# Rows of y scattered straight to their expert's part of DRAM, in place of a table of lists and gathers, on one Trainium2 core

## The chip, the cores and the metric

One NeuronCore of a Trainium2 chip runs the whole kernel. The metric is the device time in microseconds (us). All data is float32.

## The reference

A Fourier filter along the sequence (GFNet mixing), followed by a mixture of experts in which every row goes to one expert:

```python
# x: (8, 2496, 256); filt_r, filt_i: (1249, 256)
X = np.fft.rfft(x, axis=1)
y = np.fft.irfft(X * (filt_r + 1j * filt_i)[None], n=2496, axis=1).reshape(19968, 256)

logits = y @ w_gate                          # (19968, 8)
e = np.argmax(logits, axis=1)                # one expert for each row
gate = softmax(logits)[arange(N), e]
h = np.maximum(y @ w1[e], 0.0)               # w1: (8, 256, 1024)
out = gate[:, None] * (h @ w2[e])            # w2: (8, 1024, 256)
```

The reference sorts the rows by expert, multiplies each expert's rows with its weights, and puts the rows back in their order.

## The kernel before

**Fourier part.** The length 2496 is split into 39 x 64 (`N1` x `N2`). For each of the 8 batches there are four stages. Stage A (`stage_a`, DFT over 39) writes `zo` tiles to `zd` in DRAM. Stage B (`stage_b`) loads `zd` back in another order, multiplies with twiddles on TensorE and with the filter in four VectorE operations. Stage C (`stage_c`) writes `uo` tiles to `ud` in DRAM. Stage D (`stage_d`) loads `ud` and makes y, four of 22 columns of 117 rows at a time, in tiles `yo`. y goes to `yd` in DRAM. `turn_y` transposes y, `logits` multiplies it with the gate weights (result in the PSUM tile `lt`), the small copy `ls` takes that out, and `turn_logits` turns it back so that `lg` holds eight logits for each row. `zo`, `uo` and `yo` are allocated from one ring of six tiles (tag `st`). Loads of x, z and u share a ring of `NIN` = 8 tiles (`fin`).

**Routing.** After the last column of a batch, `route` works on all 22 columns: maximum, one-hot `oe` of the expert, softmax sum, and the rank of each row within its expert. The rank takes two matmuls on `oe` (`rk`: one with a triangle, one with ones) and a scan. The row of `table` (a DRAM tensor with a part for each expert) is that rank plus the rows counted so far (`cnt`). For each of the 22 columns, GpSimd then scatters 117 rows of 12 bytes to the table (L512: number of the output row, gate, number of the row in `yd`). `tile_map` then computes, on VectorE, which expert and which place of the table each tile of 512, 256 or 128 rows has (`erow`, `rrow`).

**Experts.** There are 65 tiles. For each, `listed` loads the tile's part of the table to `idt` (SP reads `rrow` into a register and waits for the batch's scatters), `gather` fetches the rows of `yd` by GpSimd with one indirect DMA for each 128 rows (L613), `turn_x` transposes them (`xT`), `hidden` does 8 steps of w1 with a ReLU, and `result` does w2, multiplies by the gate from `idt` and scatters 128 rows to the output by GpSimd (L668). Weights are loaded by SP, 1 MB at a time, into two `w1t` and two `w2t` tiles. The last 128-row tiles take w2 from a resident copy `w2s`, and w1 from four tiles.

**Order.** The order of PE, VectorE (DVE), ScalarE (ACT) and SP is written out by the program. `slot(k)` lists the steps of one time slot: stages B and C of batch k, stage A of batch k + 1, stage D and the logits of batch k - 1, each with a cost in us. The main loop takes such a step or an expert step, by a credit and by planned due times; after each it flushes the delayed stores (`move`), starts loads, advances the routing by two pieces (`side`) and issues expert loads (`prefetch`). `either` gives a copy out of PSUM to VectorE or ScalarE by planned load. GpSimd has its own order, in which the DMAs were issued.

In the trace the slots of stage B for batches 1 and 2 run from 77.7 to 141.0 us and from 141.0 to 209.3 us; from about 1047 us on only expert work is left.

Of the kernel before, what the change touches and what calls it, by code (L numbers as in the profile page):

```python
# [19 lines left out]
P = 128  # L20
# [112 lines left out]
def kernel(  # L133
# [40 lines left out]
    YB = TP * NG  # L174
    yd = dram.tile([B * YB + 1, D], F32, tag="yd", name="yd")

    table = dram.tile([TR, 3], I32, tag="table", name="table")
# [28 lines left out]
    seg = cst.tile([P, E, NG], F32, name="seg")  # L206
    fill = cst.tile([P, 3], I32, name="fill")
    yrow = cst.tile([TP, NG], I32, name="yrow")
# [45 lines left out]
    def load_rest():  # L254
        nc.sync.dma_start(out=tds, in_=td)
        nc.vector.memset(wg, 0.0)
        nc.sync.dma_start(out=wg[:, :, :E], in_=moe_w_gate.rearrange("(i p) e -> p i e", p=P))
        nc.sync.dma_start(out=ids0, in_=ids)
        nc.sync.dma_start(out=vld, in_=valid)
        zrow = sb.tile([P, 2, D], F32, tag="yw", name="zrow")  # L260
        nc.vector.memset(zrow[:1, 0], 0.0)
        nc.sync.dma_start(out=yd[B * YB:B * YB + 1, :], in_=zrow[:1, 0])

    def make_constants():
# [5 lines left out]
        nc.gpsimd.memset(seg, 1.0)  # L270
        nc.gpsimd.memset(seg[:, :, 0:1], 0.0)
        nc.gpsimd.memset(cnt, 0.0)
        nc.gpsimd.memset(fill[:, 0:1], N)
        nc.gpsimd.memset(fill[:, 1:2], 0)
        nc.gpsimd.memset(fill[:, 2:3], B * YB)
        nc.gpsimd.iota(yrow, pattern=[[1, NG]], base=0, channel_multiplier=NG)
# [19 lines left out]
    NIN = 8  # L296
# [36 lines left out]
    def stage_a(b, c):  # L333
        i0, n = CH[c]
        xt = ins.pop(("x", b, c))
        zo = sb.tile([TP, 4, D], F32, tag="st", name="zo", bufs=6)
# [28 lines left out]
    def stage_c(b, f):  # L365
        ys = outs.pop(("y", b, f))
        j = f % 4
        if j == 0:
            outs["u", b] = sb.tile([P, 4, D], F32, tag="st", name="uo", bufs=6)
# [16 lines left out]
    def stage_d(b, c):  # L386
        if c == 0:
            lgs[b] = sb.tile([TP, NG, E], F32, tag="lg", name="lg")
        i0, n = CH[c]
        ui = ins.pop(("u", b, c))  # L390
        yo = outs["o", b, c] = sb.tile([TP, 4, D], F32, tag="st", name="yo", bufs=6)
        for j in range(0, n, 2):
            p = bank()
            for i in range(2):

                k = N1 if i0 + j + i == NG - 1 else TP
                mm(p[:TP, i * D:(i + 1) * D], lhsT=tds[:k, i0 + j + i, :], rhs=ui[:k, j + i, :],  # L397
                   start=True, stop=True)
            evac(yo[:, j:j + 2, :], p[:TP, :].rearrange("p (i d) -> p i d", i=2), 512)
        move(yd[b * YB:(b + 1) * YB, :].rearrange("(r i) d -> r i d", i=NG)[:, i0:i0 + n, :], yo[:TP, :n])  # L400

    def turn_y(b, c):
        yo = outs.pop(("o", b, c))
# [33 lines left out]
    scatters, rows_at = {}, {}  # L437


    def route(b):  # L440
        lg = lgs.pop(b)
        sh3 = (TP, NG, E)
        she = (TP, E, NG)
        mx = sb.tile([TP, NG], F32, tag="mx", name="mx", bufs=1)
        nc.vector.tensor_reduce(mx, lg, axis=AX.X, op=ALU.max)
        oh = sb.tile([TP, NG, E], F32, tag="oh", name="oh", bufs=1)
        ex = sb.tile([TP, NG, E], F32, tag="ex", name="ex", bufs=1)
# [6 lines left out]
        idx = sb.tile([TP, NG], F32, tag="idx", name="idx", bufs=1)  # L454
        nc.vector.tensor_reduce(idx, oh, axis=AX.X, op=ALU.min)

        nc.vector.tensor_tensor(idx, idx, vld, op=ALU.mult)
        yield
        oe = sb.tile([TP, E, NG], F32, tag="oe", name="oe", bufs=1)
# [3 lines left out]
        pay = sb.tile([TP, NG, 3], I32, tag="pay", name="pay", bufs=1)  # L463
        sd = sb.tile([TP, NG], F32, tag="sd", name="sd", bufs=1)
# [4 lines left out]
        mm(rk[:TP, 0, :], lhsT=tri, rhs=oef, start=True, stop=True)  # L469
        mm(rk[:, 1, :], lhsT=ones, rhs=oef, start=True, stop=True)  # L470
        nc.vector.tensor_scalar(sd, in0=sd, scalar1=1e-9, scalar2=None, op0=ALU.add)
        nc.vector.reciprocal(pay.bitcast(F32)[:, :, 1], sd)
        yield
        nc.vector.tensor_scalar(pay[:, :, 2], in0=yrow, scalar1=float(b * YB), scalar2=None, op0=ALU.add)
        nc.vector.tensor_scalar(pay[:, :, 0], in0=ids0, scalar1=float(b * S), scalar2=None, op0=ALU.add)
        run = sb.tile([P, E, NG], F32, tag="run", name="run", bufs=1)
        runf = run.rearrange("p e t -> p (e t)")
        nc.vector.tensor_tensor_scan(
            runf, seg.rearrange("p e t -> p (e t)"), rk[:, 1, :], 0.0, op0=ALU.mult, op1=ALU.add
# [3 lines left out]
        pos = sb.tile([TP, E, NG], F32, tag="ex", name="pos", bufs=1)  # L483
        posf = pos.rearrange("p e t -> p (e t)")
        nc.vector.tensor_tensor(posf, runf[:TP], rk[:TP, 1, :], op=ALU.subtract)
        nc.vector.tensor_tensor(posf, posf, rk[:TP, 0, :], op=ALU.add)
# [6 lines left out]
        rowf = sb.tile([TP, NG], F32, tag="rowf", name="rowf", bufs=1)  # L493
        nc.vector.tensor_reduce(rowf, pos.rearrange("p e t -> p t e"), axis=AX.X, op=ALU.add)
        yield
        row = sb.tile([TP, NG], U32, tag="row", name="row", bufs=1)
        nc.vector.tensor_copy(row, rowf)  # L497
        nc.vector.tensor_tensor(cnt, cnt, run[:, :, NG - 1], op=ALU.add)
        yield
        rows = [(row[:N1 if t == NG - 1 else TP, t:t + 1], pay[:N1 if t == NG - 1 else TP, t, :]) for t in range(NG)]  # L500
        if b == B - 1:
# [5 lines left out]
            nc.vector.tensor_copy(pad, padf)  # L507
            rows += [(pad[:, e:e + 1], fill) for e in range(E)]
        scatters[b] = []
        rows_at[b] = pool(now[0] + 5.0, len(rows)) + 3.0  # L510
        for t, (at, what) in enumerate(rows):
            sc = nc.gpsimd.indirect_dma_start(  # L512
                out=table,
# [8 lines left out]
            scatters[b].append(sc.ins.name)  # L522
            yield
# [62 lines left out]
    work, idt, xgs, xts, w1t, w2t, hs = [], {}, {}, {}, {}, {}, {}  # L586
# [6 lines left out]
    def listed(i):  # L593
        n, e, r, b = work[i]
        r0 = nc.sync.value_load(r, min_val=0, max_val=TR - n * P)
        idt[i] = moe.tile([P, 4, 3], I32, tag="idt", name="idt", bufs=6)
        ld = nc.sync.dma_start(
            out=idt[i][:, :n], in_=table[bass.ds(r0, n * P), :].rearrange("(p i) c -> p i c", i=n)
        )
        tc.add_to_no_dep_group("listed", ld.ins)  # L600
        for name in scatters.pop(b, ()):
            tc.add_manual_dep(
                ld.ins, name, mybir.DependencyInfo(mybir.DependencyClass.Sync, mybir.DependencyReason.DATA),
                reason="the table is written for all batches so far",
            )

    def gather(i):
        n, e, r, b = work[i]
        xgs[i] = moe.tile([P, 4, D], F32, tag="xg", name="xg")

        rows = (b + 1) * YB if b < B - 1 else B * YB + 1
        for j in range(n):
            nc.gpsimd.indirect_dma_start(  # L613
                out=xgs[i][:, j], out_offset=None, in_=yd[0:rows, :],
                in_offset=bass.IndirectOffsetOnAxis(ap=idt[i].bitcast(U32)[:, j, 2:3], axis=0),
            )

    def weights(i, second):
        if late and second and TILES[i][1] == B - 1 and late["n"] < E:

            nc.sync.dma_start(out=late["w2s"][:, late["n"]], in_=moe_w2[late["n"]])
# [4 lines left out]
        if second:  # L626
            w2t[i] = moe.tile([P, FT, D], F32, tag="w2t", name="w2t")
            nc.sync.dma_start(out=w2t[i], in_=moe_w2[bass.ds(ev, 1)].rearrange("o p i d -> p (o i) d"))
        else:
            pool = late["w1"] if i >= SHORT else moe  # L630
            w1t[i] = pool.tile([P, DH, F], F32, tag="w1t", name="w1t")
            nc.sync.dma_start(out=w1t[i], in_=moe_w1[bass.ds(ev, 1)].rearrange("o p i f -> p (o i) f"))

    def turn_x(i):
        n, xg = work[i][0], xgs.pop(i)
        xts[i] = moe.tile([P, DH, 4 * P], F32, tag="xT", name="xT", bufs=1)
# [6 lines left out]
    def hidden(i, k):  # L643
        m = work[i][0] * P
        p = bank()
        for dh in range(DH):
            mm(p[:, :m], lhsT=w1t[i][:, dh, k * P:(k + 1) * P], rhs=xts[i][:, dh, :m],  # L647
               start=(dh == 0), stop=(dh == DH - 1))
        hT = moe.tile([P, 512], F32, tag="hT", name="hT", bufs=11)
# [4 lines left out]
    def result(i, j):  # L654
        n, e, r, b = work[i]
        ids = idt[i]
# [3 lines left out]
        for k in range(FT):  # L660
            w2 = late["w2s"][:, bass.ds(ev, 1), k, :] if i >= SHORT else w2t[i][:, k, :]
            mm(p[:, :D], lhsT=hs[i][k][:, j * P:(j + 1) * P], rhs=w2, start=(k == 0), stop=(k == FT - 1))  # L662
        ys = moe.tile([P, D], F32, tag="ys", name="ys", bufs=4)
        gate = ids.bitcast(F32)[:, j, 1:2]
# [5 lines left out]
            out_offset=bass.IndirectOffsetOnAxis(ap=ids.bitcast(U32)[:, j, 0:1], axis=0),  # L670
# [9 lines left out]
    def slot(k):  # L680
# [12 lines left out]
        if k > 0:  # L693
            for c in range(nch + 3):
# [7 lines left out]
                if c >= 3 and c % 2:  # L702
                    steps.append((at + 0.04, lambda c=c: turn_logits(k - 1), None, 0.25))
            steps.append((2.0, lambda: begin_route(k - 1), None, 0.0))
# [14 lines left out]
    def begin_route(b):  # L719
        flush(True)  # L720
# [16 lines left out]
    def after(b):  # L737
        yield from route(b)
# [3 lines left out]

    def side():

        while sides:
            try:
                return next(sides[0])
            except StopIteration:
                sides.pop(0)


    got = {"list": 0, "x": 0, "w1": 0, "w2": 0}
# [3 lines left out]
    def prefetch():  # L756

        def may(what, depth):
            i = got[what]
            deep = depth if i < SHORT else 4  # L760
            return i < len(work) and i - used.get(what, used["w1"]) < deep
        def mark(what, at=None):
            when[what, got[what]] = at or now[0] + 9.0
            got[what] += 1
        if may("list", 3) and rows_at[work[got["list"]][3]] <= now[0]:
            listed(got["list"])
            mark("list", now[0] + 5.0)
        i = got["x"]
        if i < got["list"] and i - used["x"] < 2 and when["list", i] <= now[0]:
            gather(i)  # L770
            mark("x", pool(now[0], work[i][0]) + 3.5)
        for what in ("w1", "w2"):
            if got[what] < got["list"] and may(what, 2):
                weights(got[what], what == "w2")
                mark(what)
# [92 lines left out]
```

## Time and profile before

| | |
|---|---|
| median of 5 runs | 1666.57 us (1665.65 to 1671.47) |
| the profiled execution | 1665.78 us, span 1663.9 us |
| mean granted TensorE clock | 0.973 |
| PE L647 (hidden), busy | 590.3 us, 2080 instructions |
| PE L662 (result), busy | 497.9 us with w2t, 83.3 us with w2s |
| POOL indirect DMAs | 176 + 8 to the table (182.0 us), 163 gathers (157.6 us), 163 to the output (164.1 us) |
| median time to landing | table 8.3 us, gather 4.3 us, output 2.6 us |
| DMA | 296.86 MB, mean 178 GB/s |

The profile is one execution, taken by the hardware profiler. PE is TensorE's matmul queue, PEld its weight loads, POOL is GpSimd, SP the queue that issues the plain DMAs. "busy" is time in instructions; "L512" is a line of the kernel. A wait line reads "who line <- what ended the wait: us in total, times, longest". A line of the order in time gives start, length, engine, line, operation, tiles and shapes, and in brackets the idle time before it with what ended it. A float32 matmul shows as two instructions (so x2 for one matmul of 512 columns).

### The profile page before, as it was taken

Reading aid. Unit: us, or ns where it says so; the run is one execution under the profiler, and the core shown is the slowest. Engines: PE = TensorE matmul, PEld = TensorE weight load, DVE = VectorE, ACT = ScalarE, POOL = GpSimd, SP = SyncE. Lnnn points to the kernel's source line nnn. Section 1 sums busy time; section 2 is a strip of 40 time slices with the busy share of each in tenths; the row PEclk is TensorE's granted clock in tenths of the full one; section 3 lists DMA queues with packets and bytes.
Section 4 is the critical chain, followed back from the end, with each engine's and each line's share of the span. In section 5 each row is a group of like instructions: output and inputs, shape, how many; then the busy total and the mean of one; then the engine's idle time right before and its main releaser. Section 6 shows DMA issues by size and latency. Waiting matters only on the chain.

```text
span 1663.9 us, 19931 instructions
## 1 busy us (share of the span) xinstructions
PE 1567.9 (94%) x6822; PEld 1122.7 (67%) x6822; DVE 561.1 (34%) x1364; ACT 320.7 (19%) x586; POOL 505.6 (30%) x528
## 2 busy tenths in 40 slices
PE   2879779999999999999999899999999999999997
PEld 1445456778666666666776576666767678899996
DVE  0746556264632252124322222120001013334342
ACT  1333223121222222222222112112121210000000
POOL 0002343252252244122622253733322122222221
PEclk7889789999999999999999999999999999999999
DMA  8988898698785286346533543343334345545551
GB/s 304 287 270 228 228 250 278 201 231 279 225 238 194 95 228 184 126 140 170 164 125 101 164 122 110 68 152 117 137 124 159 125 159 214 191 180 180 173 174 39
DMA packets 117421, 296.86 MB, mean 178 GB/s; under 512 B 28802, under 2 KB 68868, under 8 KB 102357
## 3 DMA queue, kind: packets, MB, share of 16 engines
q1 hardware_dynamic: 95786, 253.48, 48.8%
q0 software_dynamic: 21536, 42.12, 8.0%
q8 instruction: 55, 0.90, 0.2%
q14 instruction: 44, 0.36, 0.1%
HBM read 212.83 MB, written 83.60 MB: 178 GB/s over the span
## 4 chain that ended last, share of the span: by engine, by line
PE 85%; DMA 7%; issue 3%; DVE 3%; POOL 1%; SPq 0%; ACT 0%; POOLq 0%; ACTq 0%
PE bank L662 34%; PE bank L647 33%; PE bank L397 4%; PE bank L352 3%; PE bank L376 3%; PE bank L339 2%; PE bank L640 2%; DMA zd<-zo 2%; PE bank L408 2%; DMA fin<-in_x_dram 1%; PE lt L422 1%; DMA ud<-uo 1%; DMA ht<-in_filt_dram 1%; POOL table L512 1%; DMA table<-pay,row 1%
## 5 line engine op out<-in xcount | busy, mean ns | idle before, releaser
L647 PE MATMUL bank<-xT,w1t 128*128 128x512 f32 (+2 forms) x2080 | 590.3, 437 | 0.5 <-DVE xT L234 0.3
L662 PE MATMUL bank<-w2t,hT 128*128 128x256 f32 x2240 | 497.9, 380 | 0.0
L647 PEld LDWEIGHTS bank<-xT,w1t 128*128 128x128 f32 x2080 | 340.8, 192 | 206.5 <-issue 184.5
L662 PEld LDWEIGHTS bank<-w2t,hT 128*128 128x128 f32 x2240 | 422.4, 190 | 60.8 <-issue 6.6
L668 POOL DMA_INDIRECT out_dram<-ys,idt x163 | 164.1, 1007 | 495.9 <-DVE ys L666 144.5
L512 POOL DMA_INDIRECT table<-pay,row x176 | 174.2, 990 | 316.0 <-DVE row L497 234.4
L613 POOL DMA_INDIRECT xg<-yd,idt x163 | 157.6, 967 | 333.9 <-PE bank L640 218.2
L651 ACT ACTIVATE hT<-bank 128x512 f32<-128x512 f32 (+1 forms) x229 | 135.4, 592 | 507.6 <-PE bank L647 506.2
L666 DVE TENSOR_SCALAR ys<-bank,idt 128x256 f32<-128x256 f32 x150 | 72.6, 484 | 463.5 <-PE bank L662 444.3
L650 DVE TENSOR_SCALAR hT<-bank 128x128 f32<-128x128 f32 (+1 forms) x291 | 99.1, 341 | 73.4 <-PE bank L647 72.1
L352 PE MATMUL bank<-fin,tbs 128*128 128x256 f32 (+1 forms) x320 | 92.6, 413 | 24.0 <-DMA fin<-zd 24.0
L397 PE MATMUL bank<-fin,tds 117*117 117x256 f32 (+1 forms) x352 | 92.2, 404 | 12.5 <-DMA fin<-ud 11.0
L352 PEld LDWEIGHTS bank<-fin,tbs 128*128 128x128 f32 (+1 forms) x320 | 62.1, 204 | 53.7 <-issue 44.1
L397 PEld LDWEIGHTS bank<-fin,tds 117*117 117x117 f32 (+1 forms) x352 | 66.7, 193 | 44.9 <-issue 31.6
L234 DVE COPY xT<-bank 128x512 f32<-128x512 f32 (+2 forms) x60 | 28.5, 475 | 198.5 <-PE bank L640 184.3
L339 PE MATMUL bank<-fin,tas 117*117 117x512 f32 x176 | 89.1, 633 | 6.1 <-DMA fin<-in_x_dram 6.1
L234 ACT COPY xT<-bank 128x512 f32<-128x512 f32 (+2 forms) x70 | 29.8, 433 | 313.1 <-PE bank L640 229.7
L359 DVE TENSOR_TENSOR ys<-bank,ht 128x512 f32<-128x512 f32 x80 | 55.1, 688 | 94.6 <-PE bank L352 94.6
L376 PE MATMUL bank<-ys,tcs 128*128 128x512 f32 x144 | 77.5, 621 | 9.6 <-DVE ys L362 8.9
L662 PE MATMUL bank<-w2s,hT 128*128 x368 | 83.3, 380 | 0.0
L234 ACT COPY uo<-bank 128x512 f32<-128x512 f32 x80 | 46.9, 586 | 144.7 <-PE bank L376 99.7
L662 PEld LDWEIGHTS bank<-w2s,hT 128*128 128x128 f32 x368 | 68.3, 191 | 8.2
(106 smaller groups left out, 767.7 us busy)
## 6 DMA issues: line engine op xcount, KB each, us to landing
w1t<-in_moe_w_dram SPq DMA_DIRECT2D x65, 1024.0 KB
w2t<-in_moe_w_dram SPq DMA_DIRECT2D x42, 1024.0 KB
fin<-in_x_dram SPq DMA_DIRECT2D x40, 512.0 KB
zd<-zo SPq DMA_DIRECT2D x40, 468.0 KB
fin<-ud SPq DMA_DIRECT2D x40, 468.0 KB
yd<-yo SPq DMA_DIRECT2D x40, 468.0 KB
fin<-zd SPq DMA_DIRECT2D x72, 256.0 KB
ud<-uo SPq DMA_DIRECT2D x72, 256.0 KB
```

The costliest lines, as they stand in the source:

```text
L234: either(n, lambda: nc.vector.tensor_copy(o, i), lambda: nc.scalar.copy(out=o, in_=i))
L339: mm(p[:TP, :], lhsT=tas, rhs=xt[:TP, j:j + 2, :], start=True, stop=True)
L352: mm(p[:, i * D:(i + 1) * D], lhsT=tbs[:k, f + i, :], rhs=zi[:k, j + i, :], start=True, stop=True)
L376: mm(p, lhsT=tcs[:, 1, :], rhs=ys, start=True, stop=True)
L397: mm(p[:TP, i * D:(i + 1) * D], lhsT=tds[:k, i0 + j + i, :], rhs=ui[:k, j + i, :], start=True, stop=True)
L512: sc = nc.gpsimd.indirect_dma_start(out=table, out_offset=bass.IndirectOffsetOnAxis(ap=at, axis=0), in_=what, in_offset=None,)
L613: nc.gpsimd.indirect_dma_start(out=xgs[i][:, j], out_offset=None, in_=yd[0:rows, :], in_offset=bass.IndirectOffsetOnAxis(ap=idt[i].bitcast ...
L647: mm(p[:, :m], lhsT=w1t[i][:, dh, k * P:(k + 1) * P], rhs=xts[i][:, dh, :m], start=(dh == 0), stop=(dh == DH - 1))
L650: either(m, lambda: nc.vector.tensor_scalar_max(hT[:, :m], p[:, :m], 0.0), lambda: nc.scalar.activation(hT[:, :m], p[:, :m], AF.Relu))
L651: lambda: nc.scalar.activation(hT[:, :m], p[:, :m], AF.Relu))
L662: mm(p[:, :D], lhsT=hs[i][k][:, j * P:(j + 1) * P], rhs=w2, start=(k == 0), stop=(k == FT - 1))
L668: nc.gpsimd.indirect_dma_start(out=out, out_offset=bass.IndirectOffsetOnAxis(ap=ids.bitcast(U32)[:, j, 0:1], axis=0), in_=ys, in_offset=No ...
```

## The change

Every y tile gets 16 more columns (`DR` = 272): 8 with the number of the output row, 8 with the gate. Once the rows' places are known, GpSimd scatters whole rows (1088 bytes) of `yo` to `rowsd` in DRAM, where each expert has its part. `yd`, the table, the list loads and the gathers are gone; an expert tile is one plain load of 128 x n rows from `rowsd`, and number and gate are copied out of it. `route` is called for each group of eight columns (8, 8 and 6) as soon as its logits are there, three times a batch, and first copies `rk` out of PSUM (`rks`). `yo` has a ring of its own of six tiles, held until the scatter; `zo` and `uo` share four. When six are held (`held_y`), the plan puts off stage D. Weights are loaded in halves of 512 KB, three `w1t` and three `w2t` halves (eight w1 halves in the last tiles). `NIN` is 7, `hT` has 9 tiles and not 11.

```diff
-    YB = TP * NG
-    yd = dram.tile([B * YB + 1, D], F32, tag="yd", name="yd")
-    table = dram.tile([TR, 3], I32, tag="table", name="table")
+    DR = D + 16
+    rowsd = dram.tile([TR, DR], F32, tag="rows", name="rows")
-    NIN = 8
+    NIN = 7
     def stage_a(b, c):
-        zo = sb.tile([TP, 4, D], F32, tag="st", name="zo", bufs=6)
+        zo = sb.tile([TP, 4, D], F32, tag="st", name="zo", bufs=4)
     def stage_c(b, f):
-            outs["u", b] = sb.tile([P, 4, D], F32, tag="st", name="uo", bufs=6)
+            outs["u", b] = sb.tile([P, 4, D], F32, tag="st", name="uo", bufs=4)
     def stage_d(b, c):
+        held_y[0] += 1
-        yo = outs["o", b, c] = sb.tile([TP, 4, D], F32, tag="st", name="yo", bufs=6)
+        yo = outs["o", b, c] = sb.tile([P, 4, DR], F32, tag="y", name="yo", bufs=6)[:TP]
-        move(yd[b * YB:(b + 1) * YB, :].rearrange("(r i) d -> r i d", i=NG)[:, i0:i0 + n, :], yo[:TP, :n])
-    def route(b):
+    def route(b, g):
+        t0 = 8 * g
+        w = min(8, NG - t0)
...
-        mm(rk[:TP, 0, :], lhsT=tri, rhs=oef, start=True, stop=True)
-        mm(rk[:, 1, :], lhsT=ones, rhs=oef, start=True, stop=True)
+        mm(rk[:TP, 0, :E * w], lhsT=tri, rhs=oef, start=True, stop=True)
+        mm(rk[:, 1, :E * w], lhsT=ones, rhs=oef, start=True, stop=True)
+        nc.vector.tensor_copy(rks[:TP, 0, :E * w], rk[:TP, 0, :E * w])
+        nc.vector.tensor_copy(rks[:, 1, :E * w], rk[:, 1, :E * w])
...
+        yos = [outs.pop(("o", b, c)) for c in range(2 * g, min(2 * g + 2, len(CH)))]
+        for c, yo in enumerate(yos):
+            nc.vector.tensor_scalar(yo.bitcast(I32)[:, :n, D:D + 8], in0=ids0[...], scalar1=float(b * S), ...)
+            nc.vector.tensor_copy(yo[:, :n, D + 8:], sd[...])
...
             sc = nc.gpsimd.indirect_dma_start(
-                out=table,
+                out=rowsd,
                 out_offset=bass.IndirectOffsetOnAxis(ap=at, axis=0),
...
-    def listed(i):
-    def gather(i):
+    def rows_in(i):
+        xg = xgs[i] = moe.tile([P, 4, DR], F32, tag="xg", name="xg")
+        ld = nc.sync.dma_start(
+            out=xg[:, :n], in_=rowsd[bass.ds(r0, n * P), :].rearrange("(p i) c -> p i c", i=n)
+        )
+    def weights(h, second):
+        i, k = divmod(h, 2)
+            w2t[h] = moe.tile([P, FH2, D], F32, tag="w2t", name="w2t", bufs=3)
+            w1t[h] = pool.tile([P, DH, F // 2], F32, tag="w1t", name="w1t", bufs=bufs)
     def turn_x(i):
+        nc.vector.tensor_copy(idt[i][:, :n], xg.bitcast(I32)[:, :n, D:D + 1])
+        nc.vector.tensor_copy(gts[i][:, :n], xg[:, :n, D + 8:D + 9])
     def hidden(i, k):
-        hT = moe.tile([P, 512], F32, tag="hT", name="hT", bufs=11)
+        hT = moe.tile([P, 512], F32, tag="hT", name="hT", bufs=9)
     def slot(k):
                     steps.append((at + 0.04, lambda c=c: turn_logits(k - 1), None, 0.25))
+                    steps.append((at + 0.041, lambda c=c: sides.append(route(k - 1, (c - 3) // 2)), None, 0.0))
     def side():
-        while sides:
+        while sides and not (held[0] and free["p"] > now[0] + 1.5):
     def prefetch():
+            if h < 2 * len(work) and rows_at[work[h // 2][3]] <= now[0] and (
+                    h - used[what] < (3 if h < 2 * SHORT else 8)):
+                weights(h, what == "w2")
     main loop:
+            halt = f and f[2] and f[2][0] == "u" and held_y[0] == 6
```

## The prediction

> **What bounds the kernel now.** I read the page first, then what PE waited for, then the instructions in order of time around each wait, then stretches of 10 us.
>
> ```profile
> span 1663.9 us, 19931 instructions
> ...
> PE 1567.9 (94%) x6822; PEld 1122.7 (67%) x6822; DVE 561.1 (34%) x1364; ACT 320.7 (19%) x586; POOL 505.6 (30%) x528
> ...
> PEclk7889789999999999999999999999999999999999
> DMA  8988898698785286346533543343334345545551
> ```
>
> TensorE is busy 94% of the span, and the change leaves its matmuls alone but for the small rank ones. So a gain has to come out of the 96 us in which PE stood idle and out of the first six slices (250 us), where the clock row is below 9 in five and the transfers are near full. Of the 96 us, 30 are the start (5.9 us for x, 24.0 us for the first zd round trip) and 10.7 the last output rows; the change touches neither. The rest, by what PE waited for:
>
> ```profile
> PE bank L352 <- DMA fin<-zd: 24.0, 1, 24.0
> PE rk L469 <- DVE oe L460: 13.4, 6, 2.9
> PE bank L433 <- DVE ls L234: 11.8, 3, 7.0
> PE bank L397 <- DMA fin<-ud: 11.0, 3, 5.1
> PE bank L376 <- DVE ys L362: 8.9, 9, 1.6
> ```
>
> The third row matters most. Its 7.0 us, on VectorE in order of time and then on TensorE:
>
> ```profile
> 187.01 0.69 DVE L234 COPY yo<-bank 117x512 f32<-117x512 f32 x1 [7.88 <-DMA yd<-yo]
> 187.62 0.39 DVE L234 COPY ls<-lt 128x234 f32<-128x234 f32 x1
> ```
> ```profile
> 188.06 0.78 PE L433 MATMUL bank<-ident,ls 128*117 128x128 f32 x2 [6.99 <-DVE ls L234]
> 188.63 1.91 PE L352 MATMUL bank<-fin,tbs 128*128 128x256 f32 x4
> ...
> 201.49 1.03 PE L352 MATMUL bank<-fin,tbs 128*128 128x256 f32 x4
> ```
>
> PE waits for the small copy ls, which stands in VectorE's queue behind a copy into a yo tile, which waits for a transfer out of the ring of six "st" tiles that zo, uo and yo share. After the stall the same four matmuls take 1.91 us, not 1.03: the granted clock fell. The transfers were slow because of the table:
>
> ```profile
> 110.00:120.00 10.00, 5.68 (x38) 3.42 (x37) 3.47 (x7) 2.69 (x5) 0.00 (x0) 0.95 0.94 318
> 160.00:170.00 10.00, 7.67 (x39) 5.40 (x38) 2.84 (x5) 2.60 (x5) 7.80 (x8) 1.00 1.02 216
> 170.00:180.00 10.00, 9.31 (x35) 4.55 (x34) 8.53 (x31) 2.11 (x4) 7.37 (x8) 0.66 0.90 202
> 180.00:190.00 10.00, 3.01 (x18) 2.46 (x15) 1.77 (x4) 2.11 (x4) 3.14 (x4) 0.69 1.00 219
> ```
>
> (Columns: PE, weight loads, VectorE, ScalarE, GpSimd busy; clock; DMA share; GB/s.) With the 12-byte table rows under way (155 to 184 us) full queues carry 202 to 219 GB/s; without them 318.
>
> **The change, part by part.** The instruction order of the changed kernel shows that it does what it says: no gathers, no yd writes, no list loads; 184 row scatters where 184 table scatters were; 24 pairs of rank matmuls for 8.
>
> *The yo stalls.* yo gets six tiles of its own, zo and uo share four. In the old ring the fourth yo of a batch took the tile of the second uo; that is the stall above and its twin at 119.77 us (4.32 us). In the new ring nobody in that place waits for it: the sixth zo does, several PE steps later. Removed: 4.32 + 6.99 us, and after each the slow groups, (1.91 - 1.03) + (1.91 - 1.02) + (2.86 - 1.89) = 2.74 us. Together **-16.8**. The bounds are 0 (transfers set the pace there) and -16.8; I take all, as the two slots (77.7 to 141.0 and 141.0 to 209.3 us) run at 264 and 227 GB/s where 318 was reached.
>
> *The table writes go.* The fourth zo still waits for the first uo (2.33 + 0.69 us at 169 to 172 us, then 0.72 + 1.02 + 1.35 us of slow clock: 6.1). It shortens if uo lands sooner. Bounds 0 to -6.1, half: **-3**.
>
> *The rank waits.* PE does rk two or three steps after turn_logits, and VectorE must first do mx, oh, ex, oh, usually the four stage B operations of a step between (0.69 us each), idx, idx, oe. By this rule (logits copied at 0.45 us, the old operations at 0.335 us and idx at 0.2, B no sooner than its matmuls) batch 0 has 3.44 us of PE work between and 5.36 of VectorE's, so waits 2.0 (the trace: 2.12), and the eight old waits come to 12.9 us; the trace has 13.4. With 0.2 us for operations on 64 elements (lg 117x64: 219 ns), the 24 new places give: 12 at 0; three at 0.2; 0.5; 1.1; four at 1.9 (one hidden step on either side of B); 3.0, 3.0 and 3.5 (only B and one short step between). Sum 19, so **+6.1**. Clock: four of the six old waits were followed by slow matmuls (about 1.7 us), two not; one more long wait: **+1**. Bounds: -13.4 (all covered, as in the last two batches) to 24 x 2.9 - 13.4 = +56 (none covered); I take the rule, which met the old waits.
>
> The Trainium skill, "TensorE: Matmul & The Clock Gate", Part 1, lets the clock drop only after an idle window of about 3.4 us. The trace differs: after the 2.12 us wait at 146.20 us, L352 took 1.91 us at 147.48 and 1.03 at 151.99. By the page the +1 would be 0.
>
> *More VectorE work.* A batch's routing was 23 operations, 6.3 us; now 3 x 25 at about 0.2 us: 15 us. Two copies for each of 65 tiles add some 20 us. In all about +90 us on 561. Hidden behind PE after 330 us (34% busy on the mean), but in the second full slot VectorE is busy 41.6 of 68.3 us, and its queue holds stage B and the copies that PE waits for. I allow 1 us in each of the three slots to 330 us: **+3**; bounds 0 and +10 (the routing's added time in one slot on the path).
>
> *Rank matmuls.* 8 pairs at 1.28 us (146.20 to 147.48, slow clock) become 24 at about 0.45 (estimate from L433's pairs): **+1.5**; bounds 0 and +5.
>
> *The first expert tile* stands 27 us sooner in PE's order, at what was 206.5 us and not 233.3; SP issues its rows at about 205 behind 1.5 MB of loads (5 us at 300 GB/s) and the first weights 1.2 us later. PE waits perhaps 6 + 1.5 us, where it had 3.6 for xg and 2.4 for ud: **+1.5**; bounds -6 and +8.
>
> *One late wait*, 5.14 us for fin<-ud at 932 us and 1.8 us of slow clock: SP stood behind a whole w2 load until 916 us. With halves it may not: **-2.5**, bounds 0 and -7.
>
> *At nothing.* The 163 gathers (157.6 us of POOL): GpSimd is 1% of the chain; cover, PE's work. The new wait of SP for a batch's scatters, with weights, ud writes and u loads queued behind, stands where "SPq L597 <- DMA table<-pay,row" stood (57.1 us in 12, which cost PE 3.6). Of 48 yd writes SP is freed (98 us of its waits were for yo copies). Three weight halves for two wholes: the late half of w2 has one hidden step of cover, 6.9 us for 256 rows; a gather beside a 1 MB load lands in 5. If it came 3 us late, nine such tiles would cost 27. hT 11 to 9 (8 in use) and seven "in" tiles for eight: order of loads almost the same.
>
> GpSimd writes its descriptors beside VectorE's new small copies: two scatters during the old tile_map took 1.16 and 1.50 us for 0.98, and GpSimd has room. The Trainium skill, "SBUF — State Buffer", its box on DVE blocking DMA, speaks against the change here: fp32 copies within SBUF lock GpSimd out. By the row it is 0.5 us at most a scatter, and the sum stays.
>
> **Sum:** -16.8 - 3 + 6.1 + 1 + 3 + 1.5 + 1.5 - 2.5 = -9.2. The profiled execution took 1665.78 us (span 1663.9), 0.8 under the median of 1666.57; so 1656.6, told as a median 1657.4.
>
> **The rivals.**
> *Slower: yo tiles wait for their scatter.* A tile is free when its rows have landed. The third yo of a batch is copied 18.7 us after the second rank matmul (146.20 to 164.86); rows are ready 6.3 us after it, four scatters take 5.2 (1.29 each), the copy is 1.6 later: landing has 8.8 us. For: table rows landed in 8.3 us (median, up to 10.7) here, carrying 1.4 KB; now 127 KB. Against: the out rows, 128 KB, land in 2.6 (up to 8.9), and yd's bytes leave SP's queue. At 14 us PE loses 5.2 + 2.7 in each of three slots, +24: 1681. It decides above some 12 us.
> *No change: transfers set the pace* in the two full slots, so that stalls only move: a third of the -16.8 is left, +11.2: 1668.6. For: DMA share 0.85 and 0.88. Against: the GB/s above.
> *Larger gain:* half the rank waits are covered (-12) and the late wait goes whole (-4.5): 1641.
>
> **Chances.** Main sum 0.43, slower rival 0.32 (late weight halves with it), no change 0.15, larger gain 0.10. A measurement of this kernel can tell 0.3%, 5 us. Of the main case 0.04 falls within that and 0.03 above: faster 0.46, same 0.19, slower 0.35. The range reaches from just under the larger gain to just over the slower rival's 1681, which leaves out about 0.18: 1640 to 1684. The main case's own range is 1648 to 1667.
>
> **What would show it.** Right: no PE wait for ls over 1 us, none of VectorE for yo in the first 210 us; rank waits of about 19 us, the longest 3 to 3.5, in the second half of the FFT; GB/s above 260 in the second full slot. Wrong: waits of yo copies for DMA rows, rows landing over 12 us, PE waiting for w1t or w2t, fin waits that grow by what ls lost.

## The result, and the profile after

The changed kernel takes 1673.75 us (median; 1667.95 to 1679.36), the kernel before 1668.59 us: ratio 1.003 [1.0022, 1.0037]. It is not faster by 9 us (0.6%) as forecast but slower by 5 us (0.3%). The profiled execution took 1670.7 us, with a span of 1669.0 us (before 1663.9).

The head of the page, line by line beside the one shown of before:

```profile
span 1669.0 us, 21186 instructions
...
PE 1573.3 (94%) x6886; PEld 1126.2 (67%) x6886; DVE 617.6 (37%) x1921; ACT 325.0 (19%) x608; POOL 344.0 (21%) x363
...
PEclk7999899999999999999999999999999999999999
DMA  8889787676673556433734352343344436555551
```

TensorE idles 95.7 us, where it was 96.0, and is busy 5.4 us longer. So the same idle time must come from other places. The clock cost about the same in both: the trace grants TensorE 1.00 or 0.50 of its clock, and 0.50 for 93.1 us of the kernel before and 88.8 us of the changed one. What PE waited for:

```profile
PE rk L467 <- DVE oe L459: 26.3, 12, 5.4
PE bank L343 <- issue: 23.3, 1, 23.3
PE rk L467 <- DVE sd L463: 9.6, 4, 2.9
PE bank L367 <- DVE ys L353: 8.0, 8, 1.6
PE bank L389 <- DMA fin<-ud: 7.7, 2, 6.0
PE bank L330 <- DMA fin<-in_x_dram: 5.4, 1, 5.4
PE rk L467 <- ACT yt L231: 5.2, 1, 5.2
...
PE bank L424 <- DVE ls L231: 0.6, 1, 0.6
```

The ls waits (for VectorE) fell from 11.8 to 0.6 us, and the waits for xg (3.6) and zo (3.8) are gone. The three rk lines are the rank matmuls: 41.1 us in 17 waits, where they were 13.4 in 6. One of them, on VectorE in order of time and then on TensorE:

```profile
182.33 0.15 DVE L599 TENSOR_TENSOR done<-done,take 1x8 f32<-1x8 f32 x1
182.41 0.20 DVE L444 TENSOR_REDUCE mx<-lg 117x8 f32<-117x64 f32 x1
182.65 0.23 DVE L447 TENSOR_TENSOR oh<-lg,mx 117x64 f32<-117x64 f32 x1
182.79 0.69 DVE L350 TENSOR_TENSOR ys<-bank,ht 128x512 f32<-128x512 f32 x1
...
186.36 0.23 DVE L459 TENSOR_TENSOR oe<-idx,em 117x64 f32<-117x64 f32 x1
```
```profile
180.00 1.21 PE L389 MATMUL bank<-fin,tds 117*117 117x256 f32 x4
186.65 0.65 PE L467 MATMUL rk<-oe,tri 117*117 117x64 f32 x2 [5.43 <-DVE oe L459]
187.09 0.64 PE L468 MATMUL rk<-oe,ones 117*128 117x64 f32 x2
187.52 2.02 PE L367 MATMUL bank<-ys,tcs 128*128 128x512 f32 x2
```

VectorE does not stand still here. It works off the tile map of the batch before (22 operations on one partition, 177.8 to 182.5 us), then the first piece of the group's routing (mx, oh), the four operations of stage B, and the other pieces. In PE's order rk follows on half a stage D, and PE stands. The pair and the stage C behind it then run at the slow clock (2.02 us for L367, elsewhere 1.02).

On some chips the kernel before took 1667 to 1673 us (call them A), on others 1789 to 1803 us (B). So times are compared within one kind, and ratios are always to the kernel before on the same chip. No chip was measured at two times, so whether a chip keeps its kind is not known.

### The profile page after: what moved, and what is told of

The parts are those of the page before. It is cut to its first block, busy times and chain, and to the rows that moved or that the text cites. A ratio compares the mean times of both kernels' runs of the same rounds, so it can differ in the third digit from the quotient of the medians.

```text
span 1669.0 us, 21186 instructions
## 1 busy us (share of the span) xinstructions
PE 1573.3 (94%) x6886; PEld 1126.2 (67%) x6886; DVE 617.6 (37%) x1921; ACT 325.0 (19%) x608; POOL 344.0 (21%) x363
## 4 chain that ended last, share of the span: by engine, by line
PE 87%; DVE 7%; DMA 4%; issue 1%; ACT 0%; SPq 0%; POOLq 0%; POOL 0%; DVEq 0%; ACTq 0%
PE bank L677 33%; PE bank L663 33%; PE bank L389 4%; PE bank L330 4%; PE bank L343 3%; PE bank L367 3%; PE bank L656 2%; PE bank L399 2%; PE lt L413 1%; DMA zd<-zo 1%; DVE yw L352 1%; DVE yw L351 1%; DVE ys L350 1%; DVE ys L353 1%; DMA ht<-in_filt_dram 1%
## 5 line engine op out<-in xcount | busy, mean ns | idle before, releaser
L677 PE MATMUL bank<-w2t,hT 128*128 128x256 f32 x2240 | 500.0, 380 | 0.0
L677 PEld LDWEIGHTS bank<-w2t,hT 128*128 128x128 f32 x2240 | 423.8, 191 | 63.6 <-issue 9.3
L683 POOL DMA_INDIRECT out_dram<-ys,idt x163 | 159.3, 977 | 940.1 <-DVE ys L681 443.7
L526 POOL DMA_INDIRECT rows<-yo,row x176 | 175.3, 996 | 377.5 <-issue 221.9
L667 ACT ACTIVATE hT<-bank 128x512 f32<-128x512 f32 (+1 forms) x241 | 140.2, 582 | 495.6 <-PE bank L663 495.6
L681 DVE TENSOR_SCALAR ys<-bank,gts 128x256 f32<-128x256 f32 x145 | 70.2, 484 | 429.4 <-PE bank L677 429.4
L666 DVE TENSOR_SCALAR hT<-bank 128x128 f32<-128x128 f32 (+1 forms) x279 | 94.0, 337 | 70.1 <-PE bank L663 70.1
L343 PE MATMUL bank<-fin,tbs 128*128 128x256 f32 (+1 forms) x320 | 88.7, 399 | 23.4 <-issue 23.3
L330 PE MATMUL bank<-fin,tas 117*117 117x512 f32 x176 | 93.0, 656 | 5.5 <-DMA fin<-in_x_dram 5.4
L343 PEld LDWEIGHTS bank<-fin,tbs 128*128 128x128 f32 (+1 forms) x320 | 60.2, 198 | 55.3 <-issue 46.2
L389 PE MATMUL bank<-fin,tds 117*117 117x256 f32 (+1 forms) x352 | 87.5, 388 | 7.7 <-DMA fin<-ud 7.7
L367 PE MATMUL bank<-ys,tcs 128*128 128x512 f32 x144 | 78.7, 630 | 8.0 <-DVE ys L353 8.0
L677 PE MATMUL bank<-w2s,hT 128*128 x368 | 83.2, 380 | 0.0
L677 PEld LDWEIGHTS bank<-w2s,hT 128*128 128x128 f32 x368 | 68.3, 191 | 8.2
L330 PEld LDWEIGHTS bank<-fin,tas 117*117 117x117 f32 x176 | 35.1, 203 | 40.9 <-issue 35.6
```

The source lines that it names most:

```text
L330: mm(p[:TP, :], lhsT=tas, rhs=xt[:TP, j:j + 2, :], start=True, stop=True)
L343: mm(p[:, i * D:(i + 1) * D], lhsT=tbs[:k, f + i, :], rhs=zi[:k, j + i, :], start=True, stop=True)
L367: mm(p, lhsT=tcs[:, 1, :], rhs=ys, start=True, stop=True)
L526: sc = nc.gpsimd.indirect_dma_start(out=rowsd, out_offset=bass.IndirectOffsetOnAxis(ap=at, axis=0), in_=what, in_offset=None,)
L666: either(m, lambda: nc.vector.tensor_scalar_max(hT[:, :m], p[:, :m], 0.0), lambda: nc.scalar.activation(hT[:, :m], p[:, :m], AF.Relu))
L667: lambda: nc.scalar.activation(hT[:, :m], p[:, :m], AF.Relu))
```

## The experiments

Theory 1: the gain came, and the 24 rank pairs gave it back, as they stand too near behind VectorE's work. Theory 2: transfers or VectorE set the pace, and the rank wait is only where PE meets it. Theory 3: PE's longer busy time is the loss. Theory 4 came later: the 12-byte rows cost time by themselves.

### Rank matmuls later in PE's order

```diff
+        asked_at = now[0]
+        while now[0] < asked_at + 3.0:      # 6.0 in the second run
+            yield
         rk = psr.tile([P, 2, E * NG], F32, tag="rk", name="rk")
```

With 3 us (run twice, on two chips of kind B):

> The changed kernel with one edit: the rank matmuls of a group are put in TensorE's order no sooner than 3 us of planned PE work after VectorE's oe is put in its order (it was one or two loop steps). Theory 1 (the gain of the private yo tiles came, and the 24 rank pairs gave it back by waiting for VectorE): of the 41.1 us of rank waits in the profile of the changed kernel what is over 3 us stays, 2.4 + 2.2 + 0.4 + 0.3 + 0.1 = 5.4 us, so PE idles about 35 us less; with a little of it found again in other waits, 1638 to 1650 us, about 1644, against 1674 for the changed kernel and 1668.6 for the one before. Theory 2 (transfers and VectorE's queue set the pace, the rank wait is only where PE meets it): the rank waits go and waits for fin, ys and lt grow by as much, 1668 to 1676. Theory 3 (PE's own longer busy time, 5.3 us, is the loss): 1668 to 1674 too, but with the rank waits gone and the idle time moved nowhere, which can't both be.

> The changed kernel with the rank matmuls 3 us later, again, on a chip where the kernel before takes about 1670 us (its first run was on the one where that takes 1803). Theory 1: 1646 us as there, ratio 0.983 to 0.988, between the changed kernel (0.9993 on the last such chip, 1.003 over all) and the version with VectorE's operations early as well (0.9754).

With 6 us:

> The same with 6 us. The longest rank wait in the profile of the changed kernel is 5.43 us, so Theory 1 has no rank wait left over 0.5 us: about 5 us better than with 3 us, 1632 to 1648, unless the later row scatters hold up the yo tiles or the first expert tile (then a wait of VectorE or ScalarE for rows of 2 us or more, and a time above that of 3 us). Theory 2: 1668 to 1678.

Measured: 1646.14 us (1644.18 to 1648.0) and, on the second chip, 1642.85 us; with 6 us 1665.07 us. The ratios (0.9132, 0.918, 0.9232) say little, as the kernel before took 1803 and 1789 us there. The changed kernel itself was run on a chip of kind B, and on another of kind A, as a control:

> The changed kernel itself. On a chip where the kernel before takes about 1669 us: ratio 0.999 to 1.004, as before. On one where that takes about 1795 us: if 8 scatters in a row leave it undisturbed, as they did its versions with later rank matmuls (1646 and 1643 us), 1668 to 1678 us, ratio 0.93; if those were quick for another reason, 1700 to 1800.

> The changed kernel itself, as a control beside the others, since the kernel before took 1802.8 us on the chip of the last runs against 1668.6 us in its first runs. Theory 1 (the loss of the changed kernel is its rank waits, which the 3 us edit took away; the chip did it no good): 1668 to 1678 us here too, 22 to 32 us above the version with the later rank matmuls. If that chip is quicker for any version of the changed kernel: 1640 to 1655, and then the 3 us edit has shown nothing.

Measured: 1692.79 us on B (ratio 0.9427 [0.9398, 0.9456]), above the 1668 to 1678 expected for an undisturbed run, and 1672.19 us on A (0.9993 [0.9974, 1.0012]). So 3 us of distance take 47 to 50 us off on B (on different chips of that kind), and the version is under every run of the changed kernel on either kind. In its first profile not one rk wait is left, where the changed kernel's on B has 43.2 us of them; PE idles 27 us less (108.1 to 80.9) and is busy 18 us less (1581.3 to 1563.6). So 16 us came back as other waits, mostly for ud and ys: Theory 2 holds for that part alone, and Theory 3 is out. The distance alone was not run on A.

With 6 us, 19 us come back on the same chip. A stall of 10.3 us is the largest part, first on TensorE, then on ScalarE and GpSimd:

```profile
174.61 2.06 PE L330 MATMUL bank<-fin,tas 117*117 117x512 f32 x2 [10.33 <-DMA ud<-uo]
```
```profile
173.97 0.58 ACT L231 COPY yo<-bank 117x512 f32<-117x512 f32 x1 [10.27 <-issue]
```
```profile
163.65 0.98 POOL L529 DMA_INDIRECT rows<-yo,row  x1 [23.37 <-issue]
...
167.52 0.99 POOL L529 DMA_INDIRECT rows<-yo,row  x1 [0.30 <-issue]
```

The profile names a store of uo, but ScalarE and VectorE both stand until 173.97 us before a copy into a yo tile, some 5.5 us after the fourth scatter of the group, and PE goes on 0.6 us later. The trace does not tell when these rows landed, but the time fits the "slower" rival of the prediction: copies into yo wait for their rows. In the changed kernel no such copy waits over 1.8 us; with the group routed 6 us later it is this stall.

### VectorE's pieces earlier

The seven operations from mx to sd are issued at once behind the logits' copy, not two a step:

```diff
-steps.append((at + 0.041, lambda c=c: sides.append(route(k - 1, (c - 3) // 2)), None, 0.0))
+steps.append((at + 0.041, lambda c=c: begin_group(k - 1, (c - 3) // 2), None, 0.0))
+    def begin_group(b, g):
+        r = route(b, g)        # its first yield now stands behind sd; oe and sd have two buffers
+        next(r)
+        sides.append(r)
```

With the 3 us of distance kept, on the chip of the control (A):

> The version with the rank matmuls 3 us later, but with VectorE's operations for a group (mx to sd) put in its order at once behind the logits' copy, not two pieces a step, so that rk, the scatters and the release of the yo tiles come two to four steps sooner at the same distance between oe and rk. Theory 1: rank waits below 3 us and the waits of PE for copies of yo (4.5 us there) go: 1636 to 1646. If VectorE now stands still for the logits' copy and holds up stage B: ys waits grow over 15 us and the time to 1646 to 1660.

Without it, on the chip of the second 3 us run (B):

> VectorE's operations of a group put in its order at once behind the logits' copy, but the rank matmuls only one side step behind them, with no 3 us of planned PE work between. If the place on TensorE is what counts (a chain of seven small operations behind the copy takes VectorE about 1.9 us, and one step covers 0.4 to 1.7 us): rank waits of 10 to 30 us, ratio 0.982 to 0.995. If the place on VectorE counts (the pieces stood behind stage B and the tile map): rank waits below 6 us and a ratio of 0.972 to 0.980, as with the 3 us, or better for the sooner scatters.

Measured: 1631.25 us with the distance (the early version from here on), ratio 0.9754 [0.9726, 0.9781], 41 us under the changed kernel on the same chip and somewhat better than expected; without the distance 1700.28 us (0.9497 [0.9458, 0.9535]), 57 us above the 3 us version on the same chip. The first beats both kernels on its chip. Its head and waits:

```profile
span 1628.6 us, 21214 instructions
...
PE 1557.9 (96%) x6886; PEld 1116.3 (69%) x6886; DVE 615.9 (38%) x1927; ACT 322.4 (20%) x602; POOL 345.7 (21%) x363
```
```profile
PE bank L343 <- issue: 23.2, 1, 23.2
PE bank L367 <- DVE ys L353: 15.0, 10, 4.9
...
PE rk L467 <- DVE oe L456: 1.2, 1, 1.2
```

Against the control on that chip, the rk waits went from 41.0 to 1.2 us; 12 us of it came back, mostly as waits for ys, so that PE idles 27.5 us less, and it is busy 18.1 us less (1576.0 to 1557.9). The second number is the clock's: it was granted at 0.50 for 97.0 us of the control and for 58.4 us here, which is 19 us of work at full speed. The version without the distance shows it at a single wait, on TensorE and then in stretches of 5 us (columns as in the prediction, the clock third from the end):

```profile
602.27 0.39 PE L467 MATMUL rk<-oe,tri 117*117 117x64 f32 x2 [2.31 <-DVE sd L460]
602.50 0.39 PE L468 MATMUL rk<-oe,ones 117*128 117x64 f32 x2
602.72 1.72 PE L343 MATMUL bank<-fin,tbs 128*128 128x256 f32 x4
604.23 4.71 PE L677 MATMUL bank<-w2t,hT 128*128 128x256 f32 x16
608.78 1.02 PE L367 MATMUL bank<-ys,tcs 128*128 128x512 f32 x2
609.63 3.62 PE L677 MATMUL bank<-w2t,hT 128*128 128x256 f32 x16
```
```profile
600.00:605.00 5.00, 2.73 (x10) 2.38 (x11) 3.42 (x16) 0.45 (x2) 0.00 (x0) 0.80 0.64 211
605.00:610.00 5.00, 5.00 (x19) 3.86 (x18) 4.10 (x15) 0.64 (x2) 0.27 (x1) 0.86 0.00 0
```

After 2.31 us of waiting, the clock is 0.50 from 603.0 us on for 3.4 us and 1.00 again after that. L343 takes 1.72 us and not 1.03, and L677 4.71 and not 3.62: the wait cost 2.3 us and the clock behind it 1.8. That version has 30.7 us of rk waits in 17, nearly all of about 2 us. Against the 3 us version on its chip PE idles 33 us more (110.5 to 77.8) and is busy 35 us more (1594.9 to 1560.0). So VectorE's order alone brings nothing (1700 us, where the changed kernel took 1693 on another chip of kind B); what counts is the distance on PE. The expectation nearly had the waits (10 to 30 us) but put the time below the changed kernel's; it had no price for the clock.

### The same distance in the kernel before

> The kernel before with its eight rank pairs 3 us later and nothing else. Theory 1: 13.4 us of waits go, -10 to -16 us, ratio 0.990 to 0.994. Theory 2 (transfers set the pace and the idle time moves): ratio 0.997 to 1.002.

Measured: 1690.8 us, ratio 1.0131 [1.0106, 1.0156]. All of its rk waits are gone, and it is slower by 22 us. On TensorE and GpSimd:

```profile
267.79 1.09 PE L643 MATMUL bank<-ident,xg 128*128 128x128 f32 x4 [34.07 <-DMA xg<-yd,idt]
```
```profile
231.52 0.99 POOL L515 DMA_INDIRECT table<-pay,row  x1 [40.92 <-DVE cnt L501]
...
260.04 0.89 POOL L515 DMA_INDIRECT table<-pay,row  x1 [0.30 <-issue]
261.24 0.98 POOL L616 DMA_INDIRECT xg<-yd,idt  x1 [0.30 <-issue]
```

The gather of the first expert tile had stood between the second and the third table scatter of batch 1; 3 us later it stands behind all 22 of them, 29 us of GpSimd's queue. Theory 1's 13 us came, but the waits for xg grew by 31 us, those for zd by 10 and those for ls by 4. The changed kernel has no gather in GpSimd's order, as the rows of a tile come by SP; so it can take the 3 us, which the kernel before in this order cannot, and its own time does not show that gain. With 6 us, on B, the kernel before came to 1778.28 us (0.9856 [0.9824, 0.9889]), but the stalls told of further down differ too between these two, so nothing is read from it:

> The kernel before with the same edit (6 us), where eight rank pairs wait 13.4 us in six waits. Theory 1: those go, and with them the slow matmuls after four of them (1.7 us): -10 to -15 us, ratio 0.991 to 0.994. Theory 2: within 4 us of the kernel before, ratio 0.998 to 1.002.

### The yo ring and the row size, one by one

The ring alone in the kernel before (three yo tiles of their own; and, first, four on a chip of kind B):

```diff
-        zo / uo / yo: tag="st", bufs=6
+        zo / uo: tag="st", bufs=4;  yo: tag="y", bufs=3        # 4 in the first run
-    NIN = 8, hT bufs=11
+    NIN = 7, hT bufs=10                                        # 9 in the first run
```

> The kernel before with yo in four tiles of its own beside four for zo and uo (as in the changed kernel seven tiles for loads in place of eight and nine hT for eleven make the room). Everything else, the 12-byte table, the gathers, the whole weights, one routing a batch, is as before. By the step of the prediction that put 16.8 us on the yo stalls: the ls waits (11.8 us) fall below 1.5 us and the time to 1650 to 1658, ratio 0.989 to 0.994. If transfers set the pace there: the ls waits go, fin waits grow, ratio 0.997 to 1.002. If seven load tiles for eight cost something of their own: above 1.002.

> The kernel before with three tiles of its own for yo beside four for zo and uo (seven load tiles for eight and ten hT for eleven make the room); table, gathers, weights and routing as before. The step of the prediction says -16.8 us for the yo stalls: ratio 0.990. Theory 4 (the stalls are long because the 12-byte rows hold up the transfers they wait for): with the table left, only part comes, -4 to -11 us, ratio 0.993 to 0.998, and the stall at 120 us (4.3 us), where no table row is under way, goes for certain.

Measured: 0.9934 [0.9915, 0.9953] (1791.53 us) on B, where the stalls told of below may share in it; 1668.39 us and 0.9987 [0.997, 1.0004] on A. On A the waits for ls are gone (0.5 us), and these have grown:

```profile
PE bank L352 <- DMA fin<-zd: 26.7, 3, 25.2
PE bank L397 <- DMA fin<-ud: 23.8, 7, 10.2
PE bank L339 <- DMA fin<-in_x_dram: 11.6, 6, 5.4
```

They were 24.0, 11.0 and 6.1: 21 us more, for 11.3 us of ls, 3.9 us of rk and 2.7 us of xg waits less. So the stalls only moved. That the transfers set the pace in these slots fits, but the edit also takes one of eight load tiles, and this run does not tell the two apart; three yo tiles are also fewer than the changed kernel's six. Then the transfers, with table rows of 512 bytes (the source runs on past its three words; the lists still load three):

```diff
-    table = dram.tile([TR, 3], I32, tag="table", name="table")
+    table = dram.tile([TR, 128], I32, tag="table", name="table")
-        ... pay[:TP, t, :]
+        ... payw[:TP, 3 * t:3 * t + 128]                       # hT bufs=10
```

> The kernel before with 512-byte table rows in place of 12-byte ones (the source is a piece of the same tile that runs on past its three words; the lists still load three words a row; hT has ten tiles in place of eleven to make the room). Theory 4: on a chip where the kernel before takes 1803 us it falls to 1660 to 1690; on one where it takes 1668 us it gains 3 to 12 us, ratio 0.993 to 0.998. If the size of the writes is not what matters (the number of rows, the gathers or the loads do): ratio 0.998 to 1.003 in either case.

Measured: 1654.8 us, 0.9899 [0.9874, 0.9924], 18.5 us by the medians where 3 to 12 were expected, and that while more bytes move (307 MB for 297). Of the 12.8 us between the two profiled spans (1663.9 and 1651.1), 4.3 are idle time of TensorE and 8.5 busy time. In stretches of 10 us (columns as before):

```profile
160.00:170.00 10.00, 7.04 (x31) 4.74 (x30) 3.69 (x9) 4.03 (x8) 7.56 (x8) 0.96 0.97 324
170.00:180.00 10.00, 7.73 (x39) 4.12 (x39) 6.99 (x28) 2.70 (x5) 7.86 (x8) 0.84 1.00 317
180.00:190.00 10.00, 10.00 (x40) 6.53 (x44) 6.12 (x10) 3.48 (x6) 0.94 (x2) 0.85 0.91 315
```

The same stretches carry 315 to 324 GB/s (the scatters end at 181.3 us), where 12-byte rows left 202 to 219. The stall of 6.99 us is 2.27 us now; the one at 120 us, before any table row, is as long as it was (4.01). The Trainium skill, "DMA: Bandwidth & Descriptors", Specifications, puts line rate at transfers of 512 bytes and more and has smaller ones read, changed and written back; the runs agree at these two sizes and show the price.

Both together, and both with the rank pairs 3 us later:

> The same with 512-byte table rows. If the two gains (the ring, and the 18.5 us of the wide rows alone) overlap, as both shorten the stall at 188 us: -20 to -28 us, ratio 0.983 to 0.988. If they add up as the prediction's terms would (16.8 more): -35 us, ratio 0.979. If the ring brings nothing beside wide rows: ratio 0.988 to 0.991.

> The same with the eight rank pairs 3 us later. Theory 1: their 13.4 us of waits go too (the longest is 2.9 us) and with them slow matmuls behind them: another -12 to -18 us, about 1628 to 1640 where the kernel before takes 1670. It also says how much the rows scattered straight to the experts bring by themselves, against the best version of the changed kernel (ratio 0.9754): if this comes to 0.975 to 0.980, almost nothing.

Measured: 0.9897 [0.9875, 0.9919], so the ring (again with one load tile fewer) adds nothing beside wide rows either; and 1.0026 [1.0011, 1.0041], with 24.53 us of waiting for the first xg, as above. How far the old routes can go with the gather moved was not tried.

### Twice the scatters

To price small rows in the changed kernel, every row scatter of the 3 us version was followed by a second one, of 12 bytes a row, or of the whole row, to a place that nobody reads:

```diff
+            nc.gpsimd.indirect_dma_start(out=tabled, out_offset=..., in_=what[:, D + 6:D + 9], in_offset=None)   # or in_=what
```

> The changed kernel with the rank matmuls 3 us later (1646.1 us) and, after every row scatter, a second scatter of 12 bytes a row into a table that nobody reads: the writes that the change took away, put back with nothing that waits for them. Theory 4 (small writes cost time by themselves, by holding up other transfers): on a chip where the kernel before takes about 1668 us, +5 to +20 us, with GB/s near 210 to 230 while they run; on a chip where it takes 1803 us, +50 to +130 us with TensorE idle for no releaser that the profile shows. If they cost only GpSimd's time: within 4 us of 1646.

> The changed kernel with the rank matmuls 3 us later and a second scatter of the same whole rows (1088 bytes each) into a place that nobody reads, where the run with +51 us had a second scatter of 12 bytes a row. If that cost was the second scatter's time on GpSimd (10 us more a group until the yo tiles are free): again +35 to +60 us, 1680 to 1706. If it was the size of the rows: +10 to +25 us for 22 MB more of full writes, 1656 to 1671.

> The changed kernel with the rank matmuls 3 us later and every row scattered twice, whole. On a chip of the slow kind 1783 to 1798 us again. On the other kind, beside 1697 us for a second scatter of 12 bytes: about the same (1685 to 1710) if the second scatter's time on GpSimd, which holds the yo tiles 10 us longer a group, was what cost; 1656 to 1671 if the 12-byte rows were.

> The kernel before with 512-byte table rows, 22 scatters in a row as before. On a chip of the slow kind: if the number in a row is what costs, 1770 to 1800 us, ratio 0.985 to 1.002; if the 12-byte rows are, 1650 to 1680 us, ratio 0.92 to 0.94. On a chip of the other kind: ratio 0.990 again.

Measured: 12 bytes 1697.07 us on A (1.0148 [1.012, 1.0176]), where "L332 <- ACT yo" has a wait of 13.0 us: copies into yo wait, as a group's scatters now take GpSimd 20 us. That is 25 us above the changed kernel on the same chip; the 3 us version was never run on A, so the price of the second scatter itself is not known there (the 51 us of an expectation compares A with B). Whole rows came to chips of kind B both times: 1791.49 and 1788.33 us, the first 149 us above the 3 us version on the same chip. So this pair does not tell row size from GpSimd's time; that the second scatter holds the yo tiles is seen, its share is open. On B, wide rows brought nothing to the kernel before (1.0015 [0.9994, 1.0036]).

What is slow on B shows in the kernel before with four yo tiles, while GpSimd issues the 22 table scatters and 8 fillers of the last batch (with four gathers and one output scatter among them) from 1134.7 us on:

```profile
1145.72 9.31 PE L662 MATMUL bank<-w2t,hT 128*128 128x256 f32 x41
1156.78 0.38 PE L662 MATMUL bank<-w2t,hT 128*128 128x256 f32 x1 [1.75 <-issue]
...
1173.64 0.59 PE L662 MATMUL bank<-w2t,hT 128*128 128x256 f32 x1 [2.22 <-issue]
```

From the 17th scatter on, PE gets one instruction every 1.4 to 2.8 us with nothing named that it waits for, at 31 to 44 GB/s (1160 to 1180 us), so not for want of bandwidth. Rows of 12, 512 and 1088 bytes show it, runs of 16 and more in a row do, runs of 8 hardly. Why, and why not on A, stays open.

## Why the prediction was wrong

- **The rank waits** are the step that failed: +6.1 forecast, +27.7 measured. The rule counted PE's work between turn_logits and rk, and took VectorE's pieces to start right behind turn_logits. But they start when `side` reaches them: the scatters of the group before, paced by GpSimd's plan, and the tile map stand ahead, and then mx to oe go out two pieces a step with rk right behind. At 131.77 us the logits are there, and mx starts at 136.65. Late in the Fourier part, with more expert steps between, the rule held: its four waits of 1.9 us are four of 1.8 in the trace. But it had 12 places without a wait (there are 7) and three of 3.0 to 3.5 us, where nine waits took 2.6 to 5.4 us, 31.6 in all. The two of 5.43 and 5.21 us stand behind tile maps, which it did not have at all. Not all nine come from a late start: at 376.40 and 413.59 us mx follows the logits at once, and PE still waits 3.30 and 2.79 us: the four operations of stage B stand in VectorE's queue, and little of PE's work stands between. The bound of +56 covered it; the choice of the rule, which eight old waits had met, was wrong, as those stood behind nothing.
- **The clock behind them** (+1) was mis-sized as well. The stretches at 0.50 behind rank waits add up to 48 us, where they were 14: some +17 us by half of the difference, an estimate. Without the waits PE was busy 18 us less. The prediction's rivals held no case in which a wait costs nearly twice its length.
- **Rank matmuls:** +1.5 forecast (8 pairs at 1.28 and 24 at 0.45 would be +0.6), 16.7 us for 9.2 measured, +7.6, with the time in which the two matmuls of a pair overlap counted once. A pair takes 0.70 us and not 0.45, partly for the slow clock; 0.54 in the early version, where one rank wait is left.
- **The yo stalls** (-16.8): that the new ring takes the wait away from PE was right, and in the changed kernel the fin waits did not grow (fin<-ud 7.7 us for 11.0). But the gain was put down to the wrong part: in the kernel before, the ring alone brings nothing (0.9987, with three yo tiles and seven load tiles), as the "no change" rival has it.
- **The table writes** (-3) were the larger gain by the same runs: 18.5 us by the medians on A when the rows are widened. The two terms together, 19.8, were nearly what the wide rows gave, by luck.
- **The slower rival** (0.32) did not come: rows land in 4.4 us (median, up to 8.8), not in 12. What made the kernel slower is another cause. That 1673.75 us lies inside the range of 1640 to 1684 is luck, as the range reached that far for this rival. One trace of it is seen: at 162.14 us a copy into yo waits 1.76 us for rows, inside the rank wait of 3.13 us. With 6 us of delay it is larger.
- **First expert tile:** +1.5 forecast; no wait for xg is left, 3.6 us less. **The late wait** (-2.5) stayed: 5.99 us for fin<-ud at 968.8 us. **VectorE:** +56 us busy and not +90; ys waits 8.0 for 8.9, so nothing for +3 here (15.0 in the early version, where PE no longer stands for rk). **GpSimd:** a row scatter takes 0.99 us (median), a table scatter took 0.98, so the forecast that VectorE's copies would not hold it up stands. **Halves:** no wait for a weight. The end, which the sum did not have, gave 4.6 us: PE's last idle time is 6.1 us and not 10.7. In the trace GpSimd's closing drain is that much shorter; why, was not looked for.
- **Sums:** the rule's places add up to 19.3, which is +5.9 and not +6.1, and half of them is 10 and not the 12 of the larger gain. Neither changes the account.
- Of the signs named: ls under 1 us, yes; GB/s above 260 in the second full slot, yes (264, from 132.6 to 204.8 us); no wait of VectorE for yo in the first 210 us, no (1.76 us); rank waits of about 19 us, no (41.1), and it was the one that decided.

## What to carry to other kernels

When an order is written by hand, price a new cross-engine hand-over by what stands ahead in the producer's queue at the place where it is really issued, not by the work that the consumer does in between; then put the consumer some microseconds later, and check what that delay holds up (here 3 us won, and 6 us lost some of it again). Count a wait of 2 us on TensorE nearly twice where the clock falls behind it. And before giving a stall's length to a ring of tiles, take away the slow transfer behind it alone: on A the ring was worth nothing, the row size 1%.

## What the runs showed of the hardware

- TensorE slowed after waits of about 2 us (2.31 us until 602.27, then a clock of 0.50 for 3.41 us). In the changed kernel ten of the fourteen rank waits over 1 us were followed by 3.41, 6.83 or 10.24 us at 0.50; four, of 1.78 to 2.79 us, were not. The window that the prediction quoted from the Trainium skill, "TensorE: Matmul & The Clock Gate", Part 1 (about 3.4 us), would have left all but two of these waits without a price; by the runs it was 18 us.
- 22 scatters of 117 rows of 12 bytes take a third off what full queues carry (202 to 219 GB/s for 315 to 324), though they move 31 KB.
- Two kinds of chips: with 16 or more indirect DMAs in a row, PE's instructions came 1.4 to 2.8 us apart on one kind, and the kernel before lost some 120 us; the changed kernel, with 8 in a row, lost 20, and with 16 in a row 149 more than its 3 us version on the same chip. So the change is worth 5.7% there and nothing on the other. The cause is open.
